# Decode attention on one core: two-head chunks with statistics laid between products, or four-head chunks in order

## The chip, the cores and the metric

The kernel runs on one core of a Trainium2 chip. A core has five engines, each with its own instruction stream: TensorE (PE in the profile, with its weight loads listed as PEld), VectorE (DVE), ScalarE (ACT), GpSimd (POOL) and SyncE (SP). Data is moved from device memory (HBM) to the on-chip buffer (SBUF) by 16 DMA engines, which serve queues of transfers that an engine's stream issues. Matrix products are written to PSUM, eight banks of 2 KB in each of 128 partitions. Engines wait for each other through semaphores.

The metric is device time in microseconds, the median of several executions. Before the change it is 1373.73 us, from three executions between 1373.66 and 1373.78.

## The reference

Two attention layers, A and B, decode one new token for each of 4 sequences. Both have 32 query heads of 128 features. A shares 8 key/value heads among them and looks only at the last 2048 positions of its cache. B has 32 key/value heads of its own and looks at all 8192 positions. Everything is bfloat16.

```
def layer(x, k_cache, v_cache, wq, wo):
    q = (x @ wq) as (batch, head, 1, 128)
    scores = einsum("bhqd,bhkd->bhqk", q, k) * 128 ** -0.5
    p = softmax(scores)
    o = einsum("bhqk,bhkd->bhqd", p, v)
    return o as (batch, 1, 32 * 128) @ wo          # 512 outputs
out = concatenate([A, B], -1)
```

B's keys are 4 x 32 x 8192 x 128 x 2 bytes = 268 MB, its values as much. A's keys and values are 17 MB each, the four weight matrices 4 MB each. All of it is read once.

## The kernel before, in words

A recorder (`_Sched`) collects each engine's operations with their waits; the engine streams are then written out, and stretches that repeat (between two calls of `mark`) become a hardware loop.

*Chunks.* The work is cut into chunks. A has 8, one for each key/value head with all four sequences. B has 64: two heads of one sequence each, 4 MB of keys and 4 MB of values. In SBUF a chunk's 128 partitions are split among its heads, so that each partition holds 128 positions of one head (the rows of a transfer are 32 KB). A chunk thus has 128 tiles of 128 rows by 128 features, in 16 groups of 8 (`TG`).

*Keys of a chunk* (`keys_part`, L747). For each group, `emit_T` (L455) has PE transpose 8 key tiles into one of three PSUM banks (`tr`); ACT copies every third group to SBUF (`kt`), DVE the others. Two groups later (`SLAG`) `emit_S` (L488) multiplies the transposed keys with the query into the score bank `sc`. B's chunks alternate between the two score banks.

*Values of a chunk* (`values_part`, L765). The values of chunk c are multiplied after the keys of chunk c+1, and the softmax statistics of chunk c+1 are laid between these products: the last scores and `stats_rowmax` (row maxima on DVE) after group 1, `stats_gmax` (L541: a transposition on PE, the maximum over partitions and a scaling on DVE) after group 6, `stats_bc` (L557: a product that broadcasts the maximum, and a copy) and `exp_B` (L568: ACT's exponentials, which also add up the row sums) after group 10. `emit_pv` (L611) multiplies 8 value tiles with the exponentials into `po`.

*Normalisation.* `norm_sum` (L636) adds up the row sums on PE and takes the reciprocal; `norm_out` (L654) scales `po` on DVE; `emit_sel` (L666) rearranges it with four products and four small copies (`zB`); `emit_fin` (L699) multiplies with the output weights `wos` and adds to `fin`, which holds the output until the end. In B they work on two chunks at a time and stand inside the keys part of later chunks. The very last chunk multiplies with weights that were rearranged beforehand (`emit_wol`, L687), and at the first B chunk an empty pass over values (`NONE`) stands in for a chunk that does not exist, so that all passes look alike.

*Transfers.* All loads are issued by SP in one order: keys of c+1, values of c, with output weights in between (`dma_kv`, L340). SP waits before it issues a transfer until the buffer that it overwrites is free, and everything behind it on SP waits too. B's keys and values have two buffers of 32 KB a partition each (`kv`, at 0 and 2, and at 4 and 6). Keys are free when the last transposition of the old chunk is done, values when its last product is (`take`, L302). The last chunk's loads are split (`LASTK`, `LASTV`).

PE waits for a landing directly: the first transposition of a chunk for its keys' semaphore (L455 and below), the first value product for the exponentials and the values.

Of the kernel before, what the change touches and what calls it, by code (L numbers as in the profile page):

```python
# [22 lines left out]
LASTK = 96  # L23
LASTV = (64, 32, 16, 8, 8)
# [21 lines left out]
class _Sched:  # L46
# [9 lines left out]
    def add(self, eng, emit, waits=(), key=None, at=None, self_inc=False):  # L56

        sig = None
        if key is not None:
            self.count[eng] += 1  # L60
            sig = ("eng_" + eng, 1)
            assert key not in self.tk, key
            self.tk[key] = ("eng_" + eng, self.count[eng])
        self.ops[eng].append((emit, tuple(waits), None if self_inc else sig, at))

# [94 lines left out]
def bass_concat_heads__sliding_block_cached__mha_block_cached__decode_kernel(  # L160
# [24 lines left out]
    for g in range(Hkv):  # L185
        chunks.append(dict(ab=0, U=NB, C=REP, g=g, NT=NB * W // P, norm=g, last=True, n0=0))
    for hp in range(HB // 2):
        for b in range(NB):
            chunks.append(dict(ab=1, U=2, C=1, hp=hp, b=b, NT=2 * SkB // P,
                               norm=Hkv + hp, last=b == NB - 1, n0=2 * b))  # L190
# [3 lines left out]
    for c, ch in enumerate(chunks):  # L194
        ch["UC"] = ch["U"] * ch["C"]
        assert ch["NT"] % TG == 0 and ch["NT"] * P * 2 <= (1 if ch["ab"] == 0 else 2) * 16384
        ch["NG"] = ch["NT"] // TG
        ch["s"] = len(groups)
        groups += [(c, g) for g in range(ch["NG"])]
        ch["s_last"] = len(groups) - 1  # L200
    NTA, NTB = chunks[0]["NT"], chunks[-1]["NT"]
    assert sum(LASTV) == NTB and NTA * 16 == 1024 and NTB * 2 <= 512 - NW

    NONE = -1
    sch = _Sched()
    with ExitStack() as es:
# [11 lines left out]
        qb = sb("qb", [P, 2, NW], BF16)  # L218
        wor = sb("wor", [P, NWO, 4 * DO], BF16)
# [11 lines left out]
        rm = sb("rm", [P, NSM, 4], F32)  # L231
        gm = sb("gm", [4, NSM, 4], F32)
# [5 lines left out]
        pm = sb("pm", [P, HB + 2, 2, 2, 4], F32)  # L238
        pbt = {0: sb("pba", [P, NPB, NTA * 16 + NW], BF16), 1: sb("pbb", [P, NPB, NTB * 2 + NW], BF16)}
        oT = sb("oT", [P, NSM, 16], BF16)  # L240
        oz = sb("oz", [P, 16], BF16)
        outsb = sb("outsb", [36, DO], BF16)
        outB = sb("outB", [P, DO // 2], BF16)
        sel4 = sb("sel4", [P, 4, P], BF16)
        back4 = sb("back4", [P, 2, 4, P], BF16)
        zA = sb("zA", [P, 2, 16], BF16)
        zB = sb("zB", [P, 16], BF16)
        wol = sb("wol", [P, 2, DO], BF16)
# [7 lines left out]
        semnames = ["eng_pe", "eng_dve", "eng_act", "eng_pool", "eng_sp", "d_x0", "d_x1", "d_o0", "d_o1"]  # L256
        semnames += ["d_h%d" % i for i in range(NH)] + ["d_vl%d" % i for i in range(len(LASTV))]
        semnames += ["d_wo%d" % i for i in range(NWO)] + ["d_wos", "d_kl"]
# [13 lines left out]
        sch.add("pool", lambda e: e.memset(rst[1][:, :], 0.0), key="c_rs0")  # L272
        for u in range(2):
            own = rst[1][u * P // 2:(u + 1) * P // 2, :].rearrange("p (b u) -> p u b", u=2)[:, u, :]
            sch.add("pool", lambda e, own=own: e.memset(own, 1.0), waits=["c_rs0"], key="c_rs" if u else None)
        sch.add("pool", lambda e: e.memset(qb[:, :, :], 0.0), waits=["c_rs"], key="c_qb")


        sch.add("pool", lambda e: e.memset(pm[:, :, :, :, :], 0.0), key="c_pm0")
        for i in range(4):  # L280
            sch.add("pool", lambda e, i=i: e.memset(pm[:, 2 + i::4, i // 2, i % 2, :], 1.0), waits=["c_pm0"], key="c_pm" if i == 3 else None)
# [5 lines left out]
        for r in range(4):  # L287
            sch.add("pool", lambda e, r=r: e.affine_select(
                out=sel4[:, r, :], in_=onesb[:, :], pattern=[[0, 4], [-4, 32]], compare_op=ALU.is_equal,
                fill=0.0, base=-r, channel_multiplier=1), waits=["c_onesb"])  # L290
        for r in range(4):
            for u in range(2):
                sch.add("pool", lambda e, r=r, u=u: e.affine_select(
                    out=back4[:, u, r, :], in_=onesb[:, :], pattern=[[1, P]], compare_op=ALU.is_equal,
                    fill=0.0, base=2 * P + P * u - r, channel_multiplier=-4), key="c_sel" if r == 3 and u == 1 else None)
# [37 lines left out]
        def dma_wos(hq):  # L333
# [4 lines left out]
                        waits=[("fin", NCA + 8 * hq - 1)] if hq else [], key=("wos", hq))  # L338

        def dma_kv(kind, c):  # L340
            ch = chunks[c]
            T = {("k", 0): A_k, ("k", 1): B_k, ("v", 0): A_v, ("v", 1): B_v}[(kind, ch["ab"])]

            at = HALF_A[kind][c % 2] if ch["ab"] == 0 else (0 if kind == "k" else 4) + 2 * (c % 2)

            if kind == "v" and c == NC - 1:
                at = 8
            waits = take((kind, c), at, 1 if ch["ab"] == 0 else 2, ("T", ch["s_last"]) if kind == "k" else ("pv", c))
            if kind == "v" and c == NCA + 1:
                waits = waits + [("pv", NONE)]  # L350
            if ch["ab"] == 0:
                src = T[:, ch["g"], SkA - W:, :].rearrange("b (pp j) d -> pp b (j d)", pp=P // NB)
                sch.add_dma("sp", lambda e: e.dma_start(kv[:, at, :], src), "d_h%d" % at, waits=waits, key=(kind, c))
                return
            src = T[ch["b"], 2 * ch["hp"]:2 * ch["hp"] + 2].rearrange("u (pp j) d -> (u pp) (j d)", pp=P // 2)
            dst = flat(at, 2)
            if kind == "v" and c == NC - 1:

                j0 = 0
                for i, n in enumerate(LASTV):  # L360
                    x = slice(j0 * P, (j0 + n) * P)
                    sch.add_dma("sp", lambda e, x=x: e.dma_start(dst[:, x], src[:, x]), "d_vl%d" % i, waits=waits, key=("vl", j0))
                    j0 += n
                return
            if kind == "k" and c == NC - 1:

                x = slice(0, LASTK * P), slice(LASTK * P, NTB * P)
                sch.add_dma("sp", lambda e: e.dma_start(dst[:, x[0]], src[:, x[0]]), "d_h%d" % at, waits=waits, key=(kind, c))
                sch.add_dma("sp", lambda e: e.dma_start(dst[:, x[1]], src[:, x[1]]), "d_kl", key="kl")
                return  # L370
            sch.add_dma("sp", lambda e: e.dma_start(dst, src), "d_h%d" % at, waits=waits, key=(kind, c))
# [4 lines left out]
        dma_kv("k", 0)  # L376
        dma_wq(1, 6)

        loads = [("k", c + 1) for c in range(NC - 1)]
        for c in range(NC):  # L380
            loads.insert(2 * c + 1, ("v", c))
        loads.remove(("v", NCA - 1))
        loads.insert(loads.index(("k", NCA)), ("v", NCA - 1))
        for kind, c in loads:
            if kind == "k" and c >= NCA and (c == NCA or (c - NCA) % 8 == 3 and c > NCA + 3):
                dma_wos((c - NCA) // 8)
            dma_kv(kind, c)
            if kind == "v" and c > NCA and (c - NCA) % 2 == 1:


                hq = max(0, c - NCA - 2) // 8
                sch.add("sp", lambda e: e.sem_inc(sems["eng_sp"], 1), waits=[("wos", hq)] + (["kl"] if c == NC - 1 else []),
                        key=("wos2", c - 2 if c > NCA + 1 else NONE), self_inc=True)
            if kind == "v" and c < NCA:
                dma_wo(c)
        sch.add("sp", lambda e: e.sem_inc(sems["eng_sp"], 1), waits=[("wos", HB // 4 - 1)], key=("wos2", NC - 1), self_inc=True)

# [5 lines left out]
        def pe_mm(o, l, r, start=True, stop=True, transpose=False, waits=(), key=None):  # L403
            if transpose:
                sch.add("pe", lambda e: e.transpose(o, l, r), waits, key)  # L405
            else:
                sch.add("pe", lambda e: e.matmul(o, l, r, start=start, stop=stop), waits, key)  # L407
# [13 lines left out]
        def emit_q(ab):  # L421
# [10 lines left out]
            if ab == 1:  # L432

                src, dst = src.rearrange("p (hp u b) -> p hp b u", b=NB, u=2), dst.rearrange("p (hp b u) -> p hp b u", b=NB, u=2)
# [10 lines left out]
        def tile_of(kind, c, j):  # L445
            at = half_of[(kind, c)]
            return flat(at, chunks[c]["NT"] // NTA)[:, j * P:(j + 1) * P]

        def ahead(c, n):

            return c - n if c - n >= NCA else NONE
# [3 lines left out]
        def emit_T(s):  # L455
# [5 lines left out]
            for t in range(TG):  # L461
                waits = []
                if t == 0:
                    waits = [("k", c), "c_identb"] if g == 0 else []
                    waits += [("ev", before)] if before is not None else []
                    if c >= NCA and c % 2 == 1 and g == LASTK // TG:
                        waits += [("wos2", ahead(c, 2))]
# [12 lines left out]
        def emit_qb(c):  # L480

            waits = ["c_qb", ("q", 0)] if c < 2 else [("S", chunks[c - 2]["s_last"])]

            n, col = (16, 16 * c) if c <= NCA else (2, NB * HQ + 2 * (c - NCA))
            sch.add("dve", lambda e, x=0: e.tensor_copy(qb[:, c % 2, 0:n], qs[:, bass.ds(x + col, n)]), at=col,
                    waits=waits + ([("q", 1)] if c == 1 else []), key=("qb", c))

        def emit_S(s):  # L488
            c, g = groups[s]
            ch = chunks[c]  # L490
            for t in range(TG):
                j = g * TG + t
                if ch["ab"] == 1:
                    bank, o0 = c % 2, 2 * j
# [4 lines left out]
                q = qb[:, c % 2, 0:n]  # L499
# [10 lines left out]
        HALVES = [(0, slice(0, P // 2)), (1, slice(P // 2, P))]  # L510
# [17 lines left out]
        def stats_rowmax(c):  # L528
# [352 lines left out]
```

## Time and profile before

| What | Value |
|---|---|
| Median of three executions | 1373.73 us |
| Span of the profiled execution (first to last instruction; the profile gives no other time of it) | 1371.8 us |
| PE busy | 1181.6 us, 86% |
| PE weight loads busy | 1137.0 us, 83% |
| DVE busy | 665.2 us, 48% |
| ACT busy | 434.7 us, 32% |
| Mean granted PE clock | 0.939 of full speed |
| Read from HBM | 587.21 MB, 428 GB/s over the span |
| PE transposes waiting for B's keys | 135.9 us, 58 times |
| SP waiting to issue B's loads, for scores / for value products | 753.4 us / 334.5 us |

Busy times count an engine's instructions; they overlap between engines. An idle engine costs something only where the end depends on it. "Line" is the line of the kernel's file; since one helper records all products, most of PE's work stands under L405 (transposes) and L407 (products), and is told apart by the tiles that it writes: `tr` transposes, `sc` scores, `po` value products, `ms` statistics, `fin` output.

### The profile page before, as it was taken

The numbers are of one execution on the slowest core, as the hardware profiler recorded it, in microseconds if no ns is written. First come the engines' busy times: TensorE is split into PE (matmuls) and PEld (weight loads), VectorE is DVE, ScalarE is ACT, GpSimd is POOL, SyncE is SP. The second block draws the span as 40 slices with busy tenths as digits, with TensorE's granted clock in tenths as the row PEclk, the third lists the DMA queues.
The fourth block names the chain that finished last, engine by engine and source line by source line (L and its number), as shares of the span: only waits on it lengthen the run. The fifth ranks groups of instructions, "written<-read, shape, count | busy, mean of one in ns | idle before, by whom it ended". The sixth has DMA issues, their size and how long they took to land.

```text
span 1371.8 us, 60419 instructions
## 1 busy us (share of the span) xinstructions
PE 1181.6 (86%) x27261; PEld 1137.0 (83%) x27263; DVE 665.2 (48%) x1498; ACT 434.7 (32%) x650; POOL 8.1 (1%) x32
## 2 busy tenths in 40 slices
PE   4888899888888988888899888888998888888988
PEld 4777799888888978888888888887898888888888
DVE  1775355444445544444455444544554445445544
ACT  1553233233323322332233222322333223233332
POOL 2000000000000000000000000000000000000000
PEclk9998899999999999999999999999999999999999
DMA  9999999999999999999999999999999999999998
GB/s 401 424 423 432 429 432 430 432 433 432 431 432 431 430 432 435 429 432 432 431 433 431 431 432 433 431 432 430 435 431 431 431 432 432 432 432 431 433 428 351
DMA packets 24108, 587.52 MB, mean 428 GB/s; under 512 B 2692, under 2 KB 2712, under 8 KB 5144
## 3 DMA queue, kind: packets, MB, share of 16 engines
q1 hardware_dynamic: 24056, 587.22, 99.7%
q8 instruction: 16, 0.26, 0.1%
q14 instruction: 4, 0.03, 0.0%
q10 hardware_dynamic: 32, 0.01, 0.0%
HBM read 587.21 MB, written 0.01 MB: 428 GB/s over the span
## 4 chain that ended last, share of the span: by engine, by line
DMA 60%; PE 38%; issue 1%; DVE 1%; ACT 0%; SPq 0%; DVEq 0%
DMA kv<-in_B_k_cache_dram 55%; PE tr L405 23%; PE sc L407 9%; PE po L407 3%; DMA kv<-in_B_v_cache_dram 2%; DMA kv<-in_B_wq_dram 2%; PE fin L407 2%; DMA kv<-in_A_k_cache_dram 1%; PE ms L407 1%; ACT kt L473 0%; DVE sA L524 0%; DVE rm L533 0%; PE ms L405 0%; PE tr L407 0%; DVE sA L522 0%
## 5 line engine op out<-in xcount | busy, mean ns | idle before, releaser
L405 PE MATMUL tr<-identb,kv 128*128 128x128 bf16 x8704 | 695.6, 230 | 140.9 <-DMA kv<-in_B_k_cache_dram 135.9
L475 DVE COPY kt<-tr 128x1024 bf16<-128x1024 bf16 x736 | 499.9, 690 | 442.8 <-PE tr L405 441.1
L405 PEld LDWEIGHTS tr<-identb,kv 128*128 128x128 bf16 x8704 | 550.8, 104 | 157.1 <-DMA kv<-in_B_k_cache_dram 106.1
L473 ACT ACTIVATE kt<-tr 128x1024 bf16<-128x1024 bf16 x352 | 359.3, 1023 | 664.5 <-PE tr L405 664.4
L407 PE MATMUL sc<-qb,kt 128*128 128x64 bf16 x8704 | 445.1, 196 | 14.1 <-ACT kt L473 12.8
L407 PEld LDWEIGHTS sc<-qb,kt 128*128 128x128 bf16 x8704 | 365.2, 100 | 25.1 <-ACT kt L473 20.2
L407 PE MATMUL po<-pbb,kv 128*128 128x64 bf16 x8320 | 283.6, 192 | 3.2 <-issue 3.0
L407 PEld LDWEIGHTS po<-pbb,kv 128*128 128x128 bf16 x8320 | 262.9, 97 | 5.4 <-issue 3.1
L574 ACT ACTIVATE pbb<-sc,negb 64x128 bf16<-64x128 f32 x128 | 51.6, 403 | 255.7 <-DVE negb L561 254.9
L538 DVE TENSOR_REDUCE rm<-sc 64x1 f32<-64x128 f32 x128 | 37.0, 289 | 55.7 <-PE sc L407 54.8
L550 DVE TENSOR_REDUCE gm<-ms 1x2 f32<-1x128 f32 (+1 forms) x72 | 20.1, 279 | 48.4 <-PE ms L405 48.4
L561 DVE COPY negb<-ms 128x1 f32<-128x1 f32 (+1 forms) x72 | 11.4, 159 | 50.2 <-PE ms L407 50.1
L407 PE MATMUL ms<-identf,gx 1*128 1x1 f32 (+1 forms) x144 | 27.2, 256 | 4.0 <-issue 3.1
L407 PEld LDWEIGHTS ms<-identf,gx 1*128 1x128 f32 (+1 forms) x144 | 21.1, 182 | 7.9 <-issue 3.3
L683 DVE CAST zB<-ms 32x16 bf16<-32x16 f32 x128 | 21.8, 170 | 11.1 <-PE ms L407 9.8
L663 DVE TENSOR_TENSOR oz<-po,rz 128x16 bf16<-128x16 f32 x33 | 5.8, 174 | 40.5 <-PE po L407 40.5
L574 ACT ACTIVATION_READ_ACCUMULATOR pbb<-sc,negb 64x1 f32 x128 | 23.7, 185 | 0.0
L407 PE MATMUL po<-pba,kv 128*128 128x64 bf16 x512 | 20.5, 199 | 3.6 <-issue 2.3
L407 PEld LDWEIGHTS po<-pba,kv 128*128 128x128 bf16 x512 | 17.9, 102 | 6.2 <-ACT pba L594 4.2
L405 PE MATMUL ms<-identf,rm 128*1 128x128 f32 (+1 forms) x72 | 19.5, 271 | 2.6 <-DVE rm L533 2.5
L407 PE MATMUL fin<-wos,zB 128*4 128x256 bf16 x256 | 19.3, 272 | 0.0
L554 DVE TENSOR_SCALAR gx<-gm 1x128 f32<-1x128 f32 (+1 forms) x72 | 15.9, 221 | 2.5
(60 smaller groups left out, 179.8 us busy)
## 6 DMA issues: line engine op xcount, KB each, us to landing
kv<-in_B_k_cache_dram SPq DMA_DIRECT2D x63, 4096.0 KB, 27.4
kv<-in_B_v_cache_dram SPq DMA_DIRECT2D x63, 4096.0 KB, 31.7
kv<-in_A_k_cache_dram SPq DMA_DIRECT2D x8, 2048.0 KB, 14.5
kv<-in_A_v_cache_dram SPq DMA_DIRECT2D x8, 2048.0 KB, 16.1
kv<-in_A_wq_dram SPq DMA_DIRECT2D x1, 4096.0 KB, 12.2
kv<-in_B_wq_dram SPq DMA_DIRECT2D x1, 4096.0 KB, 27.3
wor<-in_A_wo_dram SPq DMA_DIRECT2D x8, 512.0 KB, 9.8
wos<-in_B_wo_dram SPq DMA_DIRECT2D x8, 512.0 KB, 20.5
```

The lines of the kernel that those rows point to most:

```text
L405: sch.add("pe", lambda e: e.transpose(o, l, r), waits, key)
L407: sch.add("pe", lambda e: e.matmul(o, l, r, start=start, stop=stop), waits, key)
L473: sch.add("act", lambda e: e.activation(dst, src, ACTF.Copy), waits=waits, key=("ev", s))
L475: sch.add("dve", lambda e: e.tensor_copy(dst, src), waits=waits, key=("ev", s))
L538: sch.add("dve", lambda e, src=src, pp=pp: e.tensor_reduce(out=rm[pp, m, 0:1], in_=src, axis=AX.X, op=ALU.max), waits=[("S", ch["s_last"]) ...
L550: sch.add("dve", lambda e: e.tensor_reduce(out=gm[0:C, m, 0:U], in_=src, axis=AX.X, op=ALU.max), waits=[("trm", c)], key=("gmax", c))
L554: sch.add("dve", lambda e: e.tensor_scalar(out=dst, in0=gv, scalar1=-scale, scalar2=None, op0=ALU.mult), waits=[("gmax", c)], key=("gx", c))
L561: sch.add("dve", lambda e: e.tensor_copy(negb[:, m, 0:C], ms[:, col:col + C]), waits=[("bc", c)], key=("negb", c))
L574: sch.add("act", lambda e, src=src, pp=pp, n=n, u=u: e.activation(probs_of(c)[pp, :, u], src, ACTF.Exp, bias=negb[pp, m, 0:1], scale=scale ...
L663: sch.add("dve", lambda e: e.tensor_tensor(out=o, in0=i0, in1=i1, op=ALU.mult), waits=waits, key=("oT", c))
L683: sch.add("dve", lambda e, src=src, pp=pp: e.tensor_copy(z[pp, :].rearrange("p (r b) -> p r b", r=4), src), waits=[("sm", c)] + free if h ...
```

## The change

B's chunks become four heads of one sequence: 32 chunks of 8 MB of keys and 8 MB of values, 256 tiles in 32 groups. A partition then holds 256 positions of one head, 64 KB of keys and 64 KB of values.

- *Buffers.* Keys have one fixed buffer (`KB = 0`, four units of 16 KB) and values one (`VB = 4`). Keys are loaded in two pieces of 4 MB, each of which waits for the transposes of its own half of the chunk before; values in one piece of 8 MB with 64 KB rows, which waits for the last value product of the chunk before. The last two chunks' loads are split finer.
- *Order.* `keys_part` and `values_part` remain for A alone. A B chunk is one loop body (`whole_B`): its keys, its statistics, its exponentials, its values, its normalisation and its output product, in this order. The first half of the row maxima is taken during the keys (`rh`), the second half after them.
- *Scores.* A chunk's scores fill both banks (1024 columns). The exponentials are four, one a head, over 256 positions on 32 partitions; the buffer for them (`pbb`) and the query's (`qq`) are single.
- *Normalisation.* Once a chunk, and once for twice the heads. Of the four small copies of `emit_sel` two go to ACT.
- *Landings.* PE no longer waits for a transfer's semaphore. Pool waits for each landing and then raises `r_k` or `r_v` by the number of groups that landed; PE waits for the group that it needs (`QK`, `QV`). The wait for output weights goes with the values' relay.
- *Removed.* The empty pass over values, the rearranged weights of the last chunk (`back4`, `wol`), SP's own relay of the output weights.

The core of the diff:

```diff
-LASTK = 96
-LASTV = (64, 32, 16, 8, 8)
+LASTK = (32, 32, 64, 64, 64)
+NEXTV = (128, 64, 64)
+LASTV = (128, 64, 32, 16, 8, 8)
+QK = (0, 4, 8, 16, 24)
+QV = (0, 16, 24, 28, 30, 31)
...
+    def relay(self, eng, sems, name, n, waits):
+        self.ops[eng].append((lambda e: e.sem_inc(sems[name], n), tuple(waits), None, None))
...
-    for hp in range(HB // 2):
+    for hq in range(HB // 4):
         for b in range(NB):
-            chunks.append(dict(ab=1, U=2, C=1, hp=hp, b=b, NT=2 * SkB // P,
-                               norm=Hkv + hp, last=b == NB - 1, n0=2 * b))
+            chunks.append(dict(ab=1, U=4, C=1, hq=hq, b=b, NT=4 * SkB // P))
...
+        def dma_B(kind, c):
+            ch = chunks[c]
+            T, at, steps = (B_k, KB, QK) if kind == "k" else (B_v, VB, QV)
+            src = T[ch["b"], 4 * ch["hq"]:4 * ch["hq"] + 4].rearrange("u (pp j) d -> (u pp) (j d)", pp=P // 4)
+            dst = flat(at, 4)
+            if kind == "k":
+                pieces, fam = (LASTK, "d_lk") if c == NC - 1 else ((NTB // 2,) * 2, "d_bk")
+            else:
+                pieces, fam = (LASTV, "d_lv") if c == NC - 1 else (NEXTV, "d_nv") if c == NC - 2 else ((NTB,), "d_bv")
+            j0, unit = 0, NTB // 4
+            for i, n in enumerate(pieces):
+                waits = []
+                for u in range(j0 // unit, (j0 + n - 1) // unit + 1):
+                    waits += held[at + u]
+                x = slice(j0 * P, (j0 + n) * P)
+                sch.add_dma("sp", lambda e, x=x: e.dma_start(dst[:, x], src[:, x]), fam + str(i), waits=waits, key=(kind, c, i))
+                j0 += n
+                sch.relay("pool", sems, "r_" + kind, n // TG, [(kind, c, i)] + ([("wos", ch["hq"])] if kind == "v" and i == 0 else []))
+            for g, end in zip(steps, steps[1:] + (NTB // TG,)):
+                sch.tk[(kind + "r", c, g)] = ("r_" + kind, (c - NCA) * (NTB // TG) + end)
+            for u in range(4):
+                held[at + u] = [("T", ch["s"] + (u + 1) * unit // TG - 1) if kind == "k" else ("pv", c)]
...
+        for c in range(NCA, NC):
+            dma_B("k", c)
+            if (c - NCA) % NB == 0:
+                dma_wos((c - NCA) // NB)
+            dma_B("v", c)
...
         def exp_B(c):
+            pw = [("c_pb", 1)] + ([("pv", c - 1)] if c > NCA else [])
+            for u, pp in HEADS:
+                src = sc[pp, :, :].rearrange("p h (j u) -> p u (h j)", u=4)[:, u, :]
+                sch.add("act", lambda e, src=src, pp=pp, u=u: e.activation(
+                    probs_of(c)[pp, :, u], src, ACTF.Exp, bias=negb[pp, 0, 0:1], scale=scale, accum_out=rst[1][pp, u:u + 1]),
+                    waits=[("negb", c), "c_rs"] + rs_read[NSM] + pw, key=("exp", c) if u == 3 else None)
+            sc_read[0] = sc_read[1] = [("exp", c)]
...
+        def whole_B(c):
+            ch = chunks[c]
+            sch.mark()
+            emit_qb(c)
+            for g in range(ch["NG"]):
+                emit_T(ch["s"] + g)
+                if g >= SLAG:
+                    emit_S(ch["s"] + g - SLAG)
+                if g == ch["NG"] // 2 + SLAG + 1:
+                    stats_rowmax(c, 0)
+            for g in range(SLAG):
+                emit_S(ch["s_last"] + 1 - SLAG + g)
+            stats_rowmax(c, 1)
+            stats_gmax(c)
+            stats_bc(c)
+            exp_B(c)
+            for g in range(ch["NG"]):
+                emit_pv(c, g)
+                if g == 2:
+                    norm_sum(c)
+            norm_out(c)
+            emit_sel(c)
+            emit_fin(c)
```

## The prediction

> **What bounds the kernel now.** I read the page first (busy shares, DMA, chain), then the order of time around single chunks, then the granted clock in windows of 3.4 us. The page:
>
> ```profile
> span 1371.8 us, 60419 instructions
> PE 1181.6 (86%) x27261; PEld 1137.0 (83%) x27263; DVE 665.2 (48%) x1498; ACT 434.7 (32%) x650; POOL 8.1 (1%) x32
> ...
> DMA  9999999999999999999999999999999999999998
> ...
> HBM read 587.21 MB, written 0.01 MB: 428 GB/s over the span
> ...
> DMA 60%; PE 38%; issue 1%; DVE 1%; ACT 0%; SPq 0%; DVEq 0%
> ```
>
> The 16 DMA engines are full in every slice: the transfer of 587 MB is the time. But PE is busy 86%, so there is little room under it. Windows from one odd B chunk's first transpose to the next (two chunks, 4 MB of keys and 4 MB of values each) show the transfer's step, and windows over four chunks that followed each other without a wait for data show PE's:
>
> ```profile
> 603.85:643.98 40.13, 34.72 (x788) 33.71 (x789) 18.75 (x41) 12.05 (x18) 0.00 (x0) 0.93 1.00 431
> 643.98:682.83 38.85, 33.50 (x788) 32.50 (x789) 18.75 (x41) 12.04 (x18) 0.00 (x0) 0.94 1.00 432
> ...
> 183.35:199.86 16.51, 16.30 (x405) 15.61 (x402) 9.73 (x23) 6.06 (x10) 0.00 (x0) 1.00 1.01 435
> 199.86:215.69 15.83, 15.63 (x390) 15.37 (x390) 8.91 (x18) 5.99 (x9) 0.00 (x0) 1.00 1.00 433
> ```
>
> After the length come the busy times of PE, PEld, DVE, ACT and POOL, then clock, DMA share, GB/s. 16.8 MB take 38.85 us, and 40.13 when 0.5 MB of output weights comes in between, one time in four in the new chunks: **39.2 us of transfer per 16.8 MB**. PE needs 16.51 + 15.83 = **32.3 us** for the same, with softmax statistics laid between the products of the chunk before. So PE waits some 7 us per pair and transfer sets the end. The order of time inside a chunk gives the durations:
>
> ```profile
> 183.35 1.50 PE L405 MATMUL tr<-identb,kv 128*128 128x128 bf16 x24
> 184.75 0.41 PE L407 MATMUL sc<-qb,kt 128*128 128x64 bf16 x8
> 184.99 0.61 PE L405 MATMUL tr<-identb,kv 128*128 128x128 bf16 x8
> ...
> 185.67 0.61 PE L405 MATMUL tr<-identb,kv 128*128 128x128 bf16 x8
> ...
> 195.88 1.34 PE L407 MATMUL po<-pbb,kv 128*128 128x64 bf16 x40
> 197.06 0.27 PE L405 MATMUL ms<-identf,rm 128*1 128x128 f32 x1
> ```
>
> One group (8 transposes, 8 scores) follows the last by 0.68 us; 40 value products take 1.18 us, 29.4 ns each. Last, the clock; PE waited for keys from about 680 to 682.8 us:
>
> ```profile
> 677.90:681.30 3.40, 1.56 (x42) 1.43 (x42) 0.46 (x3) 0.91 (x4) 0.00 (x0) 1.00 1.01 434
> 681.30:684.70 3.40, 1.87 (x18) 1.87 (x19) 0.69 (x1) 0.00 (x0) 0.00 (x0) 0.50 0.98 424
> 684.70:688.10 3.40, 3.40 (x44) 3.40 (x42) 1.38 (x2) 1.02 (x1) 0.00 (x0) 0.50 1.01 434
> 688.10:691.50 3.40, 3.40 (x85) 3.40 (x83) 2.28 (x5) 1.58 (x2) 0.00 (x0) 1.00 0.99 424
> ```
>
> A window in which PE was 46% busy is followed by half clock, which lasts until a window has been full. In the window from 660.8 us PE was busy 54% and the clock stayed whole.
>
> **The change part by part, per new chunk** (four heads, 16.8 MB; 32 of them, where 64 stood).
>
> *Keys.* 32 groups: three lots of transposes first (1.64 us from 183.35 to 184.99), 28 x 0.68, the last lot 0.45: 21.1 us. The first half's four row maxima fall between evictions; DVE works 1.37 us of every 2.04 there, and the 4 x 0.29 us are made up within two rounds, while three PSUM banks hold PE's lead: nothing. The last scores wait for the last eviction (0.22 to start, 0.69, 0.06) and end 1.2 us after the last transpose.
>
> *Statistics, now with nothing of PE's beside them.* Before, the value products of the older chunk stood here; now they need this chunk's exponentials. Score drain 0.23; four maxima at 0.29 (row 289 ns; same 128 elements on half the partitions) and one combining maximum 0.2: 1.4; transposition to first read 0.36; 0.28 + 0.25 for the maximum and its scaling; broadcast to read 0.48; copy and hop 0.19. Sum 3.2. Then four exponentials of 32x256 in place of two of 64x128. No row has that form. The nearest, 64x128, starts every 0.47 us (0.27 and 0.19 for reading the sum); ACT copies of 512 and 1024 elements (597 and 1023 ns) give 0.83 ns an element, so 0.58 each; bounds 0.47 (no charge for elements) and 0.70 (double charge). 4 x 0.58 + 0.06 = 2.4. From last transpose to first value product: 1.2 + 3.2 + 2.4 = 6.8 us, 5.5 of it a gap on PE.
>
> *Values.* 256 x 29.4 ns + 0.2 for the sum's product: 7.7.
>
> *Normalising, also serial now.* Product drain to DVE 0.19, scaling 0.17, hop 0.06, selection to read 0.28, four small copies, two on DVE (0.36) and two on ACT (no row: between DVE's 0.34 for two and 0.82 for two of 256 elements; I take 0.44), hop 0.06, output product 0.53: 1.7. Loop turn 0.2 (last product to first transpose where keys were there).
>
> Sum with full clock: 21.1 + 6.8 + 7.7 + 1.7 + 0.2 = **37.5 us**, under the transfer's 39.2. That is not all: by the windows above a gap of 5.5 us always leaves some 3.4 us window less than half busy. The half clock begins inside the gap and runs on into the value products until one window has been full: 2.7 to 6.1 us of them, by where the gap falls among the windows; mean 4.4. At half clock a product takes 54 ns (8 scores in 0.43 us instead of 0.23), so 4.4 us hold 2.4 us of work: 2.0 lost. The small products of the gap and some normalisation add 0.4. **40.0 us per chunk**, over the transfer's 39.2: PE becomes the bound. The gap at the end of a chunk (1.3 us) leaves its window over 60% busy, so the transposes start at full clock.
>
> [...]
>
> *Buffers and queues.* The values' issue waits for the last value product of the chunk before, and SP's later issues queue behind it. From that product as zero: issue, about 2 us to move, values until 21.4; the two key halves are released at 13 and 23 and land at 31 and 41; the next issue comes at 40.0. The queue just does not run dry, values are 5 us early, keys are there when PE comes back. So single buffers cost nothing beyond the order, while PE is the bound; in a shorter cycle transfer is the cover. Where output weights are loaded, SP also waits for the previous chunk's output product, 1.7 us later; the 5 us cover it.
>
> *Relays.* A landing goes over Pool. No row prices it: not below nothing, at most the longest hop to issue, 3.0 us; covered by the 5 us. *64 KB rows.* 426 GB/s in the A part (16 KB rows), 432 with 32 KB: the next step at most half of 1.4% on half the bytes, 4 us of 1250; a loss is not excluded; I take 0, PE being the bound. *Removed:* the empty pass over values at the first B chunk (128 products, 3.8 us) and the folded output weights; both lie under transfer.
>
> **Sum.** First B transpose at 123.8 us as now (the A part is unchanged); 32 x 40.0 = 1280; first pass over new code 4 (the row of before: 2.98 us of issue in the first B loop, and smaller ones); output 2.7 (from 1369.1 to the end now). Span 1410.5. The profiled execution's span is 1371.8, 1.9 under the median: **1412 us**, 2.8% slower.
>
> **The rivals.** (1) *Twelve windows.* Since the clock changes at window ends only, the cycle can fall into step with them. If the serial sum is 37.9 or more (exponentials at 0.70, or a longer loop turn), 12 x 3.41 = 40.96 per chunk is a stable step: 123.8 + 1311 + 8.6 = 1443. At 37.1 it is 11.5 windows, 39.3: 1388, still my case. (2) *The clock costs nothing* or the gap is nearer 4.5 us: transfer stays the bound at 39.2, but the last chunk is no longer spread: keys of 8 MB must be transposed (21.1 against 19.4 of landing), then 6.8 and 7.7 come after: the last value product ends some 9 us after the last landing instead of 1, so 1381. (3) *Not slower:* if the serial sum, cold clock included, is under 35.5 us, PE runs ahead of the transfer at the end too, and the split last pieces leave 5 us behind the landing: 1372. For it speaks that every load is still continuous; against it that 6.8 + 1.9 us of each chunk have no other work on PE. (4) *The end-of-chunk gap also halves the clock:* another 2.5 us of each chunk: 1490.
>
> **How the numbers follow.** Forecast 1386 to 1430: 0.55; (1) 0.25; (2) 0.10; (3) 0.05; (4) 0.05. The range 1383 to 1447 leaves out (3), (4) and part of (2): under 0.2. The measurement tells 0.2% (2.7 us). Slower: all but (3) and a little of (2), 0.94; same 0.03; faster 0.03, if (3) comes with quicker 64 KB rows.
>
> **What would show it.** DMA no longer full (about 0.98 of the stretch); per chunk one gap on PE of about 5.5 us with two short products, released by ACT's exponential; hardly a wait of transposes for keys; 32 half-clock stretches that begin in that gap; chunk starts 39.3 to 41 us apart. Wrong, if chunk starts lie 39.2 apart with waits for keys, if exponentials start much closer than 0.58, or if products after the gap run at 29 ns.

## The result, and the profile after

The changed kernel takes **1446.26 us** (median of four executions, 1445.48 to 1446.97), against 1373.7 before: 1.0528 times as long, with an interval of 1.0513 to 1.0543. The profiled execution took 1446.97 us, its span is 1445.2. The lines of its page that answer to those shown of before:

```profile
span 1445.2 us, 60238 instructions
PE 1188.1 (82%) x27027; PEld 1138.4 (79%) x27027; DVE 671.6 (46%) x1463; ACT 492.2 (34%) x713; POOL 6.4 (0%) x23
...
PEclk9998888899888888898888888998888888988888
DMA  9999999999999999999999999999999999999993
...
HBM read 587.21 MB, written 0.01 MB: 406 GB/s over the span
...
PE 79%; DVE 7%; ACT 7%; issue 4%; DMA 3%; ACTq 0%; SPq 0%; DVEq 0%
```

The DMA row alone would mislead: a digit 9 stands for 90% or more. The rate shows it, 406 GB/s in place of 428, and the chain above all: transfer held 60% of it and now holds 3%, PE, DVE and ACT hold 93%. The end is now set by work that follows work.

Where it went is seen in one chunk. The order of time from the last transposes of a chunk to the first of the next (weight loads left out; brackets give the engine's idle time before and what ended it):

```profile
603.38 0.61 PE L395 MATMUL tr<-identb,kv 128*128 128x128 bf16 x8
603.83 0.64 PE L397 MATMUL sc<-qq,kt 128*128 128x64 bf16 x16
...
604.78 0.35 PE L397 MATMUL sc<-qq,kt 128*128 128x32 bf16 x8 [0.31 <-DVE kt L462]
605.17 1.19 DVE L532 TENSOR_REDUCE rh<-sc 32x1 f32<-32x128 f32 x4 [0.45 <-PE sc L397]
...
607.50 0.58 PE L397 MATMUL ms<-identf,gx 1*128 1x1 f32 x2 [0.62 <-DVE gx L551]
608.12 0.16 DVE L558 COPY negb<-ms 128x1 f32<-128x1 f32 x1 [0.67 <-PE ms L397]
608.31 0.82 ACT L569 ACTIVATE pbb<-sc,negb 32x256 bf16<-32x256 f32 x1 [4.62 <-DVE negb L558]
...
609.14 0.82 ACT L569 ACTIVATE pbb<-sc,negb 32x256 bf16<-32x256 f32 x1
...
611.69 1.46 PE L397 MATMUL po<-pbb,kv 128*128 128x64 bf16 x24 [3.61 <-ACT pbb L569]
...
613.39 8.57 PE L397 MATMUL po<-pbb,kv 128*128 128x64 bf16 x232
...
623.58 1.51 PE L395 MATMUL tr<-identb,kv 128*128 128x128 bf16 x24
```

PE's last eight transposes start at 603.38 and the last scores but eight at 603.83; the first value product comes at 611.69. The exponentials start 0.83 us apart, and PE waits 3.61 us at a stretch for them. The 232 products after that take 8.57 us, 36.9 ns each, not the 29.4 of before. The clock in windows of 3.4 us (columns as in the prediction) says why:

```profile
603.40:606.80 3.40, 1.62 (x38) 1.31 (x34) 2.63 (x7) 0.29 (x1) 0.00 (x0) 1.00 0.91 395
606.80:610.20 3.40, 0.66 (x3) 0.49 (x2) 0.65 (x3) 1.86 (x5) 0.00 (x0) 0.50 1.07 463
610.20:613.60 3.40, 1.91 (x31) 1.91 (x32) 0.03 (x1) 1.42 (x4) 0.00 (x0) 0.50 1.07 463
613.60:617.00 3.40, 3.40 (x69) 3.40 (x67) 0.33 (x2) 0.00 (x0) 0.00 (x0) 0.50 1.01 434
617.00:620.50 3.50, 3.50 (x124) 3.50 (x122) 0.00 (x0) 0.00 (x0) 0.00 (x0) 0.99 0.95 412
620.50:623.90 3.40, 2.61 (x68) 2.10 (x65) 0.68 (x4) 0.35 (x2) 0.00 (x0) 1.00 0.21 87
```

A window 48% busy is followed by half clock, which lasts until a window has been full: three windows at half clock, in every chunk. The last row shows what the longer chunk does to the transfer: the values' buffer comes free only at the last product, so near the end of a chunk the queue runs dry (share 0.21).

The starts of the chunks, read as the first transposes of each, come at 623.58, 664.54 and so on: **40.96 us** apart, chunk after chunk from the sixth on.

```profile
664.54 1.51 PE L395 MATMUL tr<-identb,kv 128*128 128x128 bf16 x24
```

The granted clock repeats with the same period:

```profile
606.80:617.04 10.24, 6.00 (x98) 5.85 (x98) 1.01 (x5) 3.28 (x8) 0.00 (x0) 0.50 1.06 458
617.04:647.76 30.72, 28.15 (x692) 27.14 (x689) 17.95 (x35) 10.58 (x12) 0.00 (x0) 1.00 0.90 378
```

The half clock lasts 10.24 us here and 6.82 in experiment 2 below, that is three windows and two of 3.41 us. So 40.96 us are twelve windows, three at half speed and nine at full. All in all, 32 chunks cost 32 x 40.96, the first chunk another 8.5 (its step is 49.4; four idle times of PE for which the profile shows no cause make up 7.6 of it) and the next four 0.5 together, and the time before and after the chunks is 123.2 + 2.4.

### The profile page after: what moved, and what is told of

Same layout as the page of the kernel before. It is cut to its first block, busy times and chain, and to the rows that moved or that the text cites. A ratio compares the mean times of both kernels' runs of the same rounds, so it can differ in the third digit from the quotient of the medians.

```text
span 1445.2 us, 60238 instructions
## 1 busy us (share of the span) xinstructions
PE 1188.1 (82%) x27027; PEld 1138.4 (79%) x27027; DVE 671.6 (46%) x1463; ACT 492.2 (34%) x713; POOL 6.4 (0%) x23
## 4 chain that ended last, share of the span: by engine, by line
PE 79%; DVE 7%; ACT 7%; issue 4%; DMA 3%; ACTq 0%; SPq 0%; DVEq 0%
PE tr L395 33%; PE po L397 22%; PE sc L397 17%; ACT pbb L569 6%; PE ms L397 3%; DVE rh L532 2%; DMA kv<-in_B_wq_dram 2%; PE fin L397 2%; DVE kt L462 2%; DMA kv<-in_A_k_cache_dram 1%; PE ms L395 1%; DVE gm L547 1%; DVE gx L551 1%; DVE sA L515 1%; ACT zB L668 1%
## 5 line engine op out<-in xcount | busy, mean ns | idle before, releaser
L395 PE MATMUL tr<-identb,kv 128*128 128x128 bf16 x8704 | 657.6, 220 | 8.6 <-issue 5.2
L395 PEld LDWEIGHTS tr<-identb,kv 128*128 128x128 bf16 x8704 | 506.1, 98 | 19.0 <-DVE qq L471 8.1
L397 PE MATMUL po<-pbb,kv 128*128 128x64 bf16 x8192 | 320.8, 210 | 117.5 <-ACT pbb L569 115.7
L397 PEld LDWEIGHTS po<-pbb,kv 128*128 128x128 bf16 x8192 | 318.5, 111 | 120.2 <-ACT pbb L569 118.3
L397 PE MATMUL sc<-qq,kt 128*128 128x64 bf16 x8192 | 397.5, 191 | 11.2 <-DVE kt L462 9.5
L397 PEld LDWEIGHTS sc<-qq,kt 128*128 128x128 bf16 x8192 | 327.9, 98 | 20.4 <-DVE kt L462 12.6
L569 ACT ACTIVATE pbb<-sc,negb 32x256 bf16<-32x256 f32 x128 | 104.6, 818 | 150.8 <-DVE negb L558 149.3
L532 DVE TENSOR_REDUCE rh<-sc 32x1 f32<-32x128 f32 x256 | 73.2, 286 | 18.3 <-PE sc L397 15.7
L569 ACT ACTIVATION_READ_ACCUMULATOR pbb<-sc,negb 32x1 f32 x128 | 31.7, 247 | 0.0
L397 PEld LDWEIGHTS sc<-qb,kt 128*128 128x128 bf16 x512 | 21.8, 101 | 1.6 <-DVE gx L551 1.1
```

The source lines that it names most:

```text
L532: sch.add("dve", lambda e, src=src, pp=pp: e.tensor_reduce(out=rh[pp, half:half + 1], in_=src, axis=AX.X, op=ALU.max), waits=[("S", ch["s" ...
L569: sch.add("act", lambda e, src=src, pp=pp, u=u: e.activation(probs_of(c)[pp, :, u], src, ACTF.Exp, bias=negb[pp, 0, 0:1], scale=scale, acc ...
```

## The experiments

All times are device times; each run was measured beside the kernel before (1373.7 to 1373.8).

**1. Keep PE busy in the gap, with small products.**

```diff
             stats_rowmax(c, 1)
+            keep_busy(44)
             stats_gmax(c)
+            keep_busy(12)
             stats_bc(c)
             exp_B(c)
+            keep_busy(128)
```

`keep_busy(n)` issues n idle products of 64 columns into a transposition bank.

> The changed kernel, with 184 products without use laid into the gap of PE between a chunk's last scores and its first value product (44 before the transposition of the maxima, 12 before the broadcast, 128 while the exponentials run; all shorter than the waits that they fill). Theory, the clock: the chunk's chain is 38.5 us at full clock and 40.96 with the half clock behind the gap; with the gap filled the clock stays whole, chunks follow each other at the transfer's 39.2 us and the time is 1378 to 1390, no half-clock stretch left in the B part. Rival, the gap itself: what costs is that PE waits for DVE and ACT, by whatever clock; the added products change nothing and the time stays at 1446.

Measured: 1876.94 us, 1.366 times before. Both cases missed, and for a reason of which neither spoke. The waits for nothing that the profile shows ("issue") grew to 24% of the chain, and the queue that fetches instructions shows what they are; first the line of this run's page, then of the page after the change:

```profile
q8 instruction: 295, 4.83, 1.0%
```

```profile
q8 instruction: 15, 0.25, 0.1%
```

280 packets more, 4.58 MB at 16.4 KB each, are nine for each of 31 repetitions and one besides: by these counts the loop's code, grown by 368 PE instructions (184 products and their weight loads), was fetched again on every pass. So this run says nothing of the clock. The idea was run again with fewer, wider products (experiment 6).

**2 and 3. Lengthen the chain by one and by two exponentials**, written to a buffer that nobody reads.

```diff
+            for k, (u, pp) in enumerate(HEADS[:1]):     # [:2] in the second
+                dst = idle[:, k, :].rearrange("p (j x) -> p j x", x=4)[pp, :, u]
+                sch.add("act", lambda e, ...: e.activation(dst, src, ACTF.Exp, ..., accum_out=idler[pp, k:k + 1]), ...)
```

> The changed kernel with a fifth exponential per chunk, into a buffer that nobody reads: 0.835 us more on the path from statistics to values, in each of 32 chunks. Theory, steps of the clock's window: the chunk keeps to 12 windows of 3.413 us, 40.96 us, as long as its chain at full clock is between about 37.9 and 39.6; 38.5 + 0.84 = 39.3 is inside, so 1444 to 1452. Rival, a plain sum: 32 x 0.835 = 27 us more, 1473.

> As before with a fifth and a sixth exponential: 1.67 us more in each chunk, 40.2 us at full clock. Theory, steps of the window: beyond the stretch in which 12 windows hold, so the chunk leaves 40.96 and the time jumps to 1470 to 1495. Rival, a plain sum: 32 x 1.67 = 53 us more than 1446, so 1499; and one exponential more must then have cost half of that.

Measured: 1448.16 us (1.0542, interval 1.0524 to 1.0559) and 1483.81 us (1.0801, 1.0783 to 1.0819). Both times lie where the theory had them, and the plain sums are refuted. The fifth exponential added less than the expectation took: PE waited 4.22 us at a stretch in place of 3.61, so 0.61 us more in a chunk, because the next exponential began 0.62 us after it and not 0.83 (why, nothing here shows). The step stayed at 40.95 all the same, and the time rose by 2 us where a plain sum of 0.61 gives 20. The clock made room, as the windows behind the first line show, all of experiment 2:

```profile
610.59 1.46 PE L399 MATMUL po<-pbb,kv 128*128 128x64 bf16 x24 [4.22 <-ACT pbb L577]
...
601.40:604.82 3.42, 1.92 (x48) 1.73 (x45) 2.49 (x6) 0.79 (x1) 0.00 (x0) 1.00 1.06 460
604.82:608.23 3.41, 0.65 (x3) 0.37 (x3) 0.84 (x5) 1.61 (x5) 0.00 (x0) 1.00 1.02 442
608.23:611.64 3.41, 1.05 (x20) 1.06 (x21) 0.00 (x0) 2.27 (x6) 0.00 (x0) 0.50 0.94 404
611.64:615.05 3.41, 3.41 (x63) 3.41 (x61) 0.36 (x2) 0.00 (x0) 0.00 (x0) 0.50 0.93 404
```

A chunk has ten windows at full speed and two at half, instead of nine and three, because the gap now begins later in a window (last transposes done 1.1 us after the window's start, not 0.6). That window was 56% busy, not 48%, and the next one kept full clock. With the sixth exponential 1.67 us were added, and the step went through 42.06, 41.45 and 42.78 in turn, 42.1 in the mean. So the length of a chunk is not its work plus a fixed price; it depends on where its gap falls among the clock's windows, and twelve windows is a step in which it stays held.

**4. Undo the order alone.** Buffers, row sizes, relays and one-chunk loops stay; the values of chunk c come after the keys of chunk c+1 again, with the statistics between the products, and SP issues K(c+1) ahead of V(c).

```diff
-            stats_gmax(c)
-            stats_bc(c)
+            values_B(c - 1, c)
             exp_B(c)
-            for g in range(ch["NG"]):
-                emit_pv(c, g)
...
+        def values_B(c, nxt):
+            for g in range(NTB // TG):
+                if c >= NCA:
+                    emit_pv(c, g)
...
+                if nxt is not None and g == 8:
+                    stats_gmax(nxt)
+                if nxt is not None and g == 14:
+                    stats_bc(nxt)
```

> The changed kernel with its order alone undone: a chunk's values are multiplied after the next chunk's keys again, with the next chunk's maximum and broadcast laid between the products, and its exponentials beside the normalisation and the first transposes. Four heads a chunk, 64 KB rows, the single fixed buffers, the relays and the loop of one chunk stay; keys of the next chunk are loaded ahead of the values. Theory, the order: PE's chain is about 21.3 + 7.7 + 2 = 31 us, transfer is the bound again, 1368 to 1380. Rival, single buffers: a load that may start only when the buffer is free leaves the transfer with gaps, whatever the order; DMA not full and 1400 or more.

Measured: 1396.6 us (1.0174, interval 1.0148 to 1.02), between the two cases. The windows show where each case holds:

```profile
300.00:1300.00 1000.00, 849.48 (x19998) 822.20 (x19995) 480.56 (x1019) 352.03 (x512) 0.00 (x0) 0.94 1.00 432
...
1340.00:1394.00 54.00, 38.06 (x977) 36.48 (x973) 17.44 (x41) 12.94 (x21) 0.00 (x0) 0.91 0.75 316
```

For 1000 us in the middle the queue was full, with single buffers, relays and 64 KB rows in place; the mean step is 39.1, transfer's own. What is lost lies mostly at the ends: a share of 0.93 to 0.98 between 100 and 300 us, and 0.75 over the last 54 us. By these shares the start loses some 11 us, and the end some 7 more than the kernel before (0.81 over its last 32 us): 18 of the 23 us. So of the change's parts it is the order that costs in the steady stretch. That the ends belong to this way of undoing it, with half as many chunks of twice the size to lag by one, is argued and not shown.

**5. The same with mended ends:** the first values issued before the second keys, half of the last values to buffers that stand free, and the values' buffer given up by quarters.

```diff
-                held[at + u] = [... if kind == "k" else ("pv", c)]
+                held[at + u] = [... if kind == "k" else ("pv", c) if u == 3 else ("pvq", c, u)]
...
+            if c == NCA:
+                dma_B("k", c + 1)
```

> The kernel with the order undone (values after the next chunk's keys), with both ends of its stretch mended: the first chunk's values are issued ahead of the second chunk's keys, the last chunk's first 4 MB of values go to a buffer that is free since the A part, and a quarter of the value buffer is released as soon as its products are done. Theory, the ends: the 21 us by which the order alone stayed above the kernel before lie in SP's order at the first B chunks (7 to 12 us) and in the last values, which waited for a whole buffer (8 to 10 us), while the stretch between moved at the transfer's step; so 1370 to 1378. Rival, single buffers lose a little at every chunk: 1390 to 1397 again.

Measured: 1395.28 us (1.016, interval 1.0146 to 1.0174); the theory missed. The time is the rival's (1390 to 1397), but not for the rival's reason, a little lost at every chunk: between 300 and 1300 us the queue's share is 1.00 here too. The end did improve (share 0.88 over the last 56 us) and the start got worse (0.85 from 140 to 200 us, 0.88 from 200 to 300, with idle times of PE of up to 7.6 us for which the profile shows no cause). What keeps the queue from filling at the start stays open.

**6. The clock, again:** 25 idle products of 512 columns (6, 2 and 17 in the same three places), 50 PE instructions more.

> The changed kernel with the gap of PE filled by 25 products of 512 columns instead of 184 of 64 (6, 2 and 17 in the three waits; 0.22 us each at full clock), so that the loop's body grows by 50 instructions and not by 368. Theory, the clock: with the body small the stalls for code of the first attempt (1877 us, 4.8 MB of instructions read in place of 0.25) go, the clock stays whole, chunks lie 39.2 us apart and the time is 1378 to 1392. Rival, the gap itself costs: 1446. Rival, any growth of the body costs: over 1500 with issue stalls.

Measured: 1380.65 us (1.0044, interval 1.0028 to 1.0059), as the theory had it; both rivals are refuted. The mean granted clock is 0.99. One chunk as a window, and its gap:

```profile
637.28:676.05 38.77, 37.08 (x810) 32.52 (x811) 18.96 (x40) 13.88 (x20) 0.00 (x0) 1.00 1.00 432
...
658.10:661.50 3.40, 2.94 (x44) 1.82 (x41) 2.58 (x7) 0.25 (x1) 0.00 (x0) 1.00 0.89 386
661.50:664.90 3.40, 3.21 (x17) 1.44 (x15) 0.65 (x3) 2.11 (x5) 0.00 (x0) 1.00 0.74 318
664.90:668.30 3.40, 3.34 (x68) 2.40 (x67) 0.36 (x2) 1.18 (x4) 0.00 (x0) 1.00 1.07 463
```

Idle work alone gives back 65.6 of the 72.6 us. Early chunks, which have data ready, follow each other by 38.37 to 38.40 us (the third to the eighth step): that is PE's serial chain at full clock. From the tenth step on it is 38.77 (40.05 where output weights come in between), with the queue full: transfer. In the chunk shown the exponentials end at 666.10 and the idle products hold PE until 666.36, so about 0.2 us of the 38.37 are theirs: **38.2 us is the serial chain of the change**, and the cold clock costs 40.96 - 38.2 = 2.8.

**7. What makes an exponential 0.82 us?** The four of a chunk were given four forms: contiguous or strided reads, contiguous or strided writes.

```diff
+                dst = probs_of(c)[pp, :, u]
+                if u in (0, 2):
+                    src = sc[pp, 0, 0:NTB]
+                if u in (1, 2):
+                    dst = pbt[1][pp, 0, 0:NTB]
```

> The changed kernel with its four exponentials in four forms, which leaves the scores and probabilities in the wrong places (the time of the instruction alone is asked): the first reads 256 scores side by side and writes every fourth place, the second reads every fourth score over both banks and writes side by side, the third reads and writes side by side, the fourth is unchanged (0.82 us each now). If reading at a stride costs, the first and third take 0.4 to 0.55 us and the second 0.8; if writing at a stride costs, the second and third are short; if it is the 32 partitions or the sum, all stay at 0.8. The chain gets shorter by 0.6 to 0.8 us in the first two cases, 37.7 to 37.9: at the edge of the 12 windows, 1405 to 1447.

The four in the order of time of this run (the reads of the sums, which stand between them, left out):

```profile
602.90 0.82 ACT L574 ACTIVATE pbb<-sc,negb 32x256 bf16<-32x256 f32 x1 [4.62 <-DVE negb L558]
603.73 0.47 ACT L574 ACTIVATE pbb<-sc,negb 32x256 bf16<-32x256 f32 x1
604.30 0.46 ACT L574 ACTIVATE pbb<-sc,negb 32x256 bf16<-32x256 f32 x1
604.87 0.82 ACT L574 ACTIVATE pbb<-sc,negb 32x256 bf16<-32x256 f32 x1
```

The first and the last write every fourth place, the second and the third write neighbouring places; the first and the third read neighbouring places. So it is the strided write that costs 0.36 us (0.82 against 0.46), and the strided read next to nothing (0.47 against 0.46). The time, from a single execution, was 1431.33 us, the step 40.5 in the mean.

**8 and 9. Towards a faster version, on the base of 6:** keys in four pieces of 2 MB; then also the selection and the output product moved into the next chunk's keys.

```diff
-                pieces, fam = ... ((NTB // 2,) * 2, "d_bk")
+                pieces, fam = ... ((NTB // 4,) * 4, "d_bk")
...
+                if g == 8 and c > NCA:      # in 9 alone
+                    emit_sel(c - 1)
+                if g == 10 and c > NCA:
+                    emit_fin(c - 1)
```

> The changed kernel with the gap filled by 25 wide products and its keys loaded in four pieces of 2 MB instead of two of 4 MB, so that a chunk's transposes can start 4.9 us earlier. Theory: what is left of the loss with a whole clock (1380.7 against 1373.8) is PE's lag at the end: the last landing is at 1369.9 us, the last value product at 1377.7, since the last chunk's 38.5 us of chain begin when PE has finished the one before. An earlier start of each chunk moves PE closer to the landings: 1374 to 1378. Rival, the rest is lost along the way (relays, single buffers): no change, 1379 to 1382.

> The kernel with the filled gap and quarter keys, and the selection and output product of a chunk moved into the next chunk's keys (after groups 8 and 10), where they stood before: 1.3 to 1.7 us less of chain in each chunk. Theory: with transfer as the bound the chain counts only at the end, so at most those 1.7 us and what PE gains on the last landings: 1372 to 1376. Rival, a sum over the chunks: 32 x 1.5 = 48 us less is impossible under the transfer's 1368, so this shows only as no gain or a loss, if the loads of output weights, which wait for the output product, are now late: 1376 to 1385.

Measured: 1383.21 us (1.007, interval 1.0057 to 1.0084) and 1394.42 us (1.0153, 1.0139 to 1.0166); both expectations missed. Pieces of 2 MB mean 16 KB key rows and four pieces instead of two, and the step at a full queue became 38.92 instead of 38.77; which of the two costs this was not separated. In the second, the first chunk is no longer like the others; PE has idle times of up to 6.0 us for which the profile shows no cause, and the queue's share falls to 0.90 between 200 and 300 us.

**10. The term that was mis-sized, put right:** each head's exponentials go to neighbouring places, and the value products read them in four stripes.

```diff
-                    probs_of(c)[pp, :, u], src, ACTF.Exp, ...
+                    pbt[1][pp, 0, u * (NTB + 16):u * (NTB + 16) + NTB], src, ACTF.Exp, ...
...
+                if c >= NCA:
+                    p = pbt[1][:, 0, :].rearrange("p (u j) -> p u j", u=4)[:, :, j:j + 16]
```

> The exponentials are written in runs of 256 neighbouring places a head instead of to every fourth place; the value products then read four stripes of 16 columns. Nothing else is changed. From the run with four forms (contiguous writes 0.46 to 0.47 us against 0.82) the serial work of a chunk is 4 x 0.36 = 1.4 us shorter, 37.0 us at full clock. Theory (the forecast's own sum was right but for the exponentials): with the cold clock's 2.0 to 2.6 us the step is 39.3 to 40.0 us, as the forecast's case had it, and the time 1392 to 1417. Rival (the step stays held at twelve clock windows whatever the chain is): 40.96, time 1444 to 1448. If striped reading slows the value products, these are longer than 29.4 ns at full clock and the time lies above 1417 by 7.5 us for each ns.

Measured: **1410.97 us** (1.0278, interval 1.0259 to 1.0296). The exponentials and the gap in the order of time:

```profile
634.12 0.47 ACT L569 ACTIVATE pbb<-sc,negb 32x256 bf16<-32x256 f32 x1 [4.41 <-DVE negb L558]
...
634.69 0.47 ACT L569 ACTIVATE pbb<-sc,negb 32x256 bf16<-32x256 f32 x1
...
636.44 1.46 PE L397 MATMUL po<-pbb,kv 128*128 128x64 bf16 x24 [2.55 <-ACT pbb L569]
```

They start 0.57 us apart, 1.06 us less in a chunk, not the 1.4 that the expectation took. The step is no longer held: 39.29, 39.86 and 40.32 in turn towards the end, 39.9 in the mean. The step's mean and the time lie inside the theory's bounds; the rival, a step held whatever the chain is, is refuted.

**11 and 12. The same with the idle products; then finer keys for the four chunks before the last.**

> The same, with the 25 idle products that kept the clock whole. Chain 37.0 us at full clock against the transfer's 38.77 (40.05 with output weights): transfer alone sets the step. Theory: the step stays at 38.77, as in the run with idle products alone, and only the end is shorter, by 1.4 us of exponentials and 1.8 us that the last chunk catches up on its landings: 1376 to 1379, against 1380.65 with idle products alone. Rival (PE was still part of the step there): the step falls under 38.7 and the time under 1374.

> The same, and the keys of the four chunks before the last come in four pieces of 2 MB instead of two of 4 MB, so that their transposes can start sooner after a landing and the last chunk is less late at its end. Pieces of 2 MB cost 0.15 us a chunk of transfer (38.92 against 38.77): 0.6 us. Theory: the last value product, which comes some 4 us after the last landing in the run before, comes 1 to 2 us after it: 1373.5 to 1377. Rival (the lateness at the end is of another kind): the time of the run before, plus 0.6 us. Faster than the kernel before, 1373.7, only if the 64 KB value rows' 2.5 us over the whole kernel are kept to the end.

Measured: 1380.58 us (1.0052, interval 1.0034 to 1.007) and 1381.99 us (1.0056, 1.0038 to 1.0074). The theories of both missed, and the edit was at fault; the rival of the second, the time of the first plus 0.6, lies within its executions (1380.0 to 1383.2). The 17 idle products take 3.84 us, and with quicker exponentials they are what PE finishes last in the gap. The chain did not get shorter; it got longer, because value products that read stripes take 31.4 ns instead of 29.4 (256 of them 8.03 against 7.53 us in the last chunk). Every chunk then takes 38.86, PE's own 38.37 + 0.49, which leaves finer keys little to catch up at the end. Trimming the idle products to the shorter gap was not run. No version here beats the kernel before.

## Why the prediction was partly right

**The time.** Slower was right; 1446.26 lies 0.7 us inside the very end of the range (1383 to 1447); that the range holds it is luck as far as the forecast goes, since the forecast case (1386 to 1430) did not come. Its first rival did, to which the prediction gave 0.25, in its own words: a serial sum of 37.9 or more, twelve windows, 40.96 per chunk, 1443.

**The step that failed** is "ACT copies of 512 and 1024 elements ... give 0.83 ns an element, so 0.58 each; bounds 0.47 ... and 0.70". An exponential starts every 0.83 us, above the upper bound. In the chunk shown, the last scores end 1.1 us after the last transpose (forecast 1.2), the statistics take 3.2 from there (3.2), and the exponentials 3.4 until the first value product (2.4). The rows chosen had the right engine, but none of them wrote every fourth place: the copies write neighbours and the exponentials of before every second place. The fourth place is 0.36 us of each exponential (experiment 7). Four exponentials put 1.0 us on the serial sum: 37.5 became 38.2, while the other terms of the sum, taken together, were 0.3 too high. Experiment 10 is nearly the kernel that the forecast priced: exponentials 0.57 apart against the 0.58 taken, products 0.5 us a chunk slower. It came out at 39.9 us a chunk and 1410.97 us; the forecast was 40.0 and 1412. That the two meet so closely is partly luck, since the slower products and the 0.3 nearly cancel.

**From 0.7 us a chunk to 34 in all.** With the forecast's mean cost of a cold clock (2.0 and 0.4) the measured chain would give 40.6; its own 37.5 gives 39.9, which it rounds to 40.0. The held step makes it 40.96, 0.96 more than forecast in each of 32 chunks: 30.7 us. The first chunks took 8.9 us more than later ones, not 4. The first transpose came 0.6 sooner. The output took 2.4 where 2.7 was taken. 1410.5 + 30.7 + 4.9 - 0.6 - 0.3 = 1445.2, the span.

**The clock** was right in its place and its condition: half clock in the gap of every chunk, whole again after one full window, transposes at full clock. Its size is near: 2.8 us in the held step against 2.4, because value products ran at half clock from 611.69 to 617.04, 5.4 us, inside the forecast's 2.7 to 6.1 and above its mean of 4.4. In experiments 2, 3 and 10, each step less its chain gives 2.1 to 2.3. Experiment 6 takes the half clock away and the time goes back to transfer's. The gap at the end of a chunk does not halve it: rival (4) is refuted (1.6 us from the last product to the next transpose, 1.9 forecast).

**What the half clock followed.** In each of the 32 chunks it followed a window in which PE was busy 1.20 to 1.63 of 3.41 us (1.63 from the fifth chunk on), as it had followed one of 1.56 of 3.40 at 677.9 before the change. A share of busy time that parts the two cases was not found: in the kernel before, a window busy 1.69 of 3.42 us (1169.41 to 1172.83) was followed by full clock and one busy 1.92 of 3.41 (1186.48 to 1189.89) by half. "Until one window has been full" is a little too strict: before the change a window busy 2.69 of 3.42 us (759.81 to 763.23) ended the half clock, and after it one busy 2.94 of 3.41 (115.28 to 118.69) did not.

**Buffers, queues, relays, rows.** All were taken at nothing, and in the chunks this held: the waits of PE after the change list none for the landing of B's keys or values and none on Pool, and in experiments 4 and 6 the queue is full with all of them in place. The bound of at most 4 us for 64 KB rows holds too: 16.8 MB take 38.77 us where the kernel before took 38.85, 2.5 us over 32 chunks. The price of a relay by itself was not measured.

**Rival (2)** (transfer sets the step, the end is no longer spread, 1381) is what experiment 6 built: 1380.65. That it is met to the microsecond is partly luck. The last value product ends 6.8 us after the last landing (1376.7 against 1369.9), "some 9 us" in the prediction, which does not show how the 9 comes about; the last landing is 1.8 us later than before the change, and the end after that product 1.1 us longer.

## What to carry to other kernels

Take an unmeasured instruction's price from a row with the same write pattern (0.82 against 0.46 us here), not only the same engine and number of elements; where no such row exists, let the bound reach to the slowest row per element. When an order puts serial vector work between products, price the clock that the gap costs (2.8 us a chunk here), and allow for a loop that holds to the clock's windows, as this one did: 0.61 us more work in a chunk cost next to nothing, and 0.56 us less, all in all, took 1.06 off the step. Before code is added to a loop, look at the fetched instruction bytes: a body that was fetched again on each pass cost 431 us here, more than anything that was to be gained.

## What the runs showed that was not expected

- A loop can be held by the clock's windows: 0.61 us more work in each of 32 chunks changed the step from 40.96 to 40.95 us; 1.67 us more changed it to 42.1; 1.06 us less, with 0.5 back on the products, to 39.9.
- A loop body that had 368 PE instructions more was fetched again on each pass, 4.83 MB of code instead of 0.25, and the program took 431 us longer than without them; with 50 more (experiment 6) it took 1380.65 us, less than without them. No run lies between the two.
- ACT's exponential of 32 x 256 takes 0.82 us when it writes every fourth 2-byte place and 0.46 to 0.47 when it writes neighbours, however it reads; reading the sum after it takes 0.25 and 0.18.
- Products of 64 columns took 31.4 ns at full clock when their moving operand was read in four stripes of 16, and 29.4 in one piece.
- The step at a full queue changed by little with the keys' pieces: 38.92 us for 16.8 MB in four pieces with 16 KB key rows, 38.77 in two with 32 KB, both with 64 KB value rows.
